# Weighted sums of a windowed attention: from pairs of units by parity to single units with up to four query blocks per matmul

## The chip, the cores and the metric

The kernel runs on one core of a Trainium2 chip. The metric is the time of one execution in device microseconds (us). The kernel before took 880.48 us in the median of three runs (876.16, 880.61 and 880.48).

## The reference

An attention with a window of 128 keys and a linear bias for each head, over 8 batches of 8 heads, 576 positions and 64 features, is followed by a two-layer network with an exact GELU. Cut to what matters:

```python
scores = (q @ k.T) / sqrt(64)                    # per batch and head, 576 x 576
scores = where(0 <= i - j < 128, scores - slope[h] * (i - j), -1e9)
attn   = softmax(scores)                         # in float32
x      = (attn @ v).transpose(0, 2, 1, 3).reshape(4608, 512)
out    = gelu(x @ w_in) @ w_out                  # w_in 512 x 2048, w_out 2048 x 512
```

## The kernel before, in words

**Units.** One unit is one batch `b` and one pair of heads `hp`, so a batch has four units. The 576 queries are cut into nine blocks of 64, and so are the keys. A query block `j` sees the key blocks `j-2`, `j-1` and `j` alone. `scores` (line 617 is its matmul) writes the products of one unit into PSUM, `biased` (line 643, VectorE) scales them and adds the bias, `softmax` takes maxima (VectorE), exponentials (line 730, ScalarE), sums, the division by them (line 740, GpSimd) and a float16 copy (line 742, ScalarE); `low_weights` (line 749, VectorE) makes the float16 remainder, and a transposing DMA from SyncE's queue puts both into the tile `et` of the unit, keys on the partitions. Every number is a sum of a high and a low float16 part, so each product takes three terms.

**Weighted sums.** `weigh` multiplies `et` with the values `vbuf` of one unit: key pair `kb` (two key blocks, 128 partitions) serves the query blocks `2kb` to `2kb+3`. One head is 64 columns of weights, so the two heads of a unit go to two halves of the PE array and run side by side. It takes up to two query blocks in a matmul (64 or 128 columns) and is used for batches 0 to 2. `weigh_two` (line 849) serves batches 3 to 7: it takes two units at once, one query block in each matmul, sorted by the parity of the block. Where half of the 128 keys of a key pair are outside the window it uses 64 partitions alone, so four such matmuls run side by side. It needs four PSUM banks at a time (three in batch 7) and the `et` of both units, and it has 192 matmuls with 192 loads of weights, for each of ten pairs of units.

**What leaves.** `leave` and `leave_two` bring the sums to the network's input `x`: a scaled float16 copy on ScalarE (lines 890 and 874) and the remainder on VectorE (`low_part`, line 302). Nine blocks of 64 do not fit a token tile of 512, so the sums of a batch go to two tiles, `t = b` and `t = b + 1`, which are called parts 0 and 1.

**The network.** Tile `t` of 512 tokens has sixteen feature blocks `h` (line 917; for tiles 4, 5, 6 and 8 seven products on sums of halves instead, `u` and `v`, line 1288 and others), GELU, and then four output blocks `o` (line 964).

**What sets the order.** Every instruction of every engine stands in an order written out by hand. `ORDER` holds the steps of tiles 0 and 1, `LATER` those of tiles 2 to 6 (with batches 3 to 7): a token such as `5Y0` runs the task `Y0` of tile `t = 5` (batch 6) to its next `yield`. `LATER_BANKS` gives each PSUM tile its bank, `LATER_ROOMS` each output room. Engines take their instructions in that order, and so does SyncE's DMA queue. The tasks of the weighted sums are `Y` and `X` in `later_tasks`:

```python
        for n in range(2):
            two = unit(b, 2 * n), unit(b, 2 * n + 1)
            made.update({f"Y{n}": weigh_two(*two), f"X{n}": leave_two(*two)})
```

Of the kernel before, what the change touches and what calls it, by code (L numbers as in the profile page):

```python
# [18 lines left out]
B, H, S, D = 8, 8, 576, 64  # L19
# [81 lines left out]
2gs K 2V 2S0 2gs 2V 2V 2gs K 2H0 3gs 2V 2H0 2B0 K 2H0 3gs 3gs 2B0 2B0 2H0 K 2H1 2B0 2B0 2g0 K 2B0 2H1 2M00 K 2H1 2B0  # L101
2H1 K K 2H2 2g1 2H2 2M00 2H2 2B0 2H2 2v 2H3 2B0 2g2 2g0 2H3 2g1 2H3 K 2H3 2M00 2M01 2H4 2g2 2H4 2g0 K 2H4 2g1 2g3 2H4
K 2g2 2H5 K 2H5 2g4 2v 2v 2v 2v 2v 2v 2S1 2g3 2M00 2v 2v 2v 2v 2g4 2g3 2H5 K 2H5 2M00 2B1 2M00 2g4 2H6 2B1 2g5 2B1 2H6
2M00 2v 2H6 2B1 2B1 2B1 2H6 2M00 2M01 2M10 2B1 2M00 2H7 2M00 2H7 2M00 2B1 2M00 2H7 2v 2M01 2v 2M00 2v 2v 2M01 2v 2g5
2H7 2v 2v 2M01 2v 2B1 2H8 2g5 2M00 2H8 2M01 2M11 2g6 2H8 2M01 2N00 2M01 2H8 2H9 2g7 2N00 2M01 2H9 2g8 2M01 2H9 2M01 K
2g6 2H9 2M01 2H10 2H10 2M10 2N01 2S2 2g7 2g6 2M10 2N01 2H10 2M10 2g8 2H10 2B2 2g9 2H11 2g7 K 2H11 2g8 2H11 2g10 2B2
2H11 2g9 2M10 2B2 2H12 2g10 2g9 2H12 2B2 K 2H12 2B2 2g11 2B2 2H12 2g10 2B2 K 2H13 2B2 2H13 2g12 2M20 2g11 2H13 2M10
2g12 2g11 2H13 K 2H14 2g12 2g13 2H14 K 2M10 2H14 2M10 K 2H14 2M11 2M10 2H15 2g13 2H15 2M10 2g13 2H15 2M10 2g14 2H15
2M10 2M10 2o0 2B2 2M21 2g15 2g14 2M10 4gs 2g15 2g14 2M11 2o0 2g15 2N10 2M11 2M11 4gs 2N10 K K 2o0 2M20 2M20 2M20 2M11
2M20 2o0 2M20 2M21 2M11 K 2M20 2M21 2M21 2M20 2M11 2M21 2M11 2M21 2M11 2M21 2o1 2k0 2M11 K 2M11 K 2N11 2M20 2S3 2N11  # L110
2M20 2M20 2o1 2B3 2M20 2M20 2B3 2B3 2Q 2M20 K 2k0 2B3 2B3 2M21 2N20 2M21 2o1 2B3 2M21 2M30 2M21 K 2M21 2B3 2B3 2o1 K
2B3 2M30 2M30 2M30 2N21 2M30 2Y0 2k1 2M31 2M30 2q 2M30 2M30 2M30 2M30 2o2 2M30 2N20 2M30 2M31 2M30 2M31 2M31 2M31 2o2
2X0 2N21 2M31 2M31 2M31 2X0 2M31 2X0 2X0 2M31 2X0 2X0 2X0 2M31 2Q 2M30 2X0 2o2 2X0 2X0 2N30 2M31 2X0 2N30 2X0 2N31 2o2
2o3 2q 2k2 2N31 2k1 2q 2q 2o3 2k2 2q 2q 2q 2q 2q 2q 2q 2q 2q 2q 2q 2q 2q 2q 2q 2o3 2q 2q 2Y1 2q K 2o3 2X1 3U 2X1 2X1
3H0 K 2X1 3H0 2k3 2X1 2X1 3H0 2X1 K 2k3 2X1 3H0 K 2X1 2X1 3H1 2X1 3g0 K 2X1 3U 3H1 K 3H1 3H1 3S0 3g1 4gs 3V 3H2 3B0
3g0 3V K 3H2 3B0 3g1 3H2 3H2 3B0 3H3 3g2 3V 3g0 3B0 3H3 K 3V 3B0 3H3 3B0 3H3 3M00 3B0 3g2 3S1 3g3 K 3B0 3M00 3g1 3H4
3B0 3g3 3H4 3B1 3M00 3H4 3M01 K 3M00 3H4 3B1 3M00 3B1 K 3H5 3M00 3g2 3B1 3g4 K 3H5 3B1 3B1 3H5 K 3M00 3H5 3g3 3B1 3M01
3g4 3H6 3B1 3M00 3H6 3M10 3B1 3M00 3H6 3M00 3g5 3M00 3g4 3H6 3M00 3M11 3H7 3M00 3H7 3v 3g6 3g5 3H7 3M00 3g6 3H7 3M01
3H8 3H8 3N00 3H8 3M01 3H8 3M01 3g5 3N00 3g7 3H9 3M01 3g6 3H9 3M01 3v 3v 3v 3M01 3v 3H9 3v 3v 3M01 3v 3g8 3v 3H9 3M01
3v 3v 3M10 3v 3M01 3v 3H10 3v 3g7 3v 3v 3v 3H10 3v 3v 3g8 3v 3H10 3g7 3M01 3H10 3g8 3M10 3H11 3M10 3N01 3M10 3H11 3M10  # L120
3N01 3H11 3M11 3M10 3M10 3H11 3M11 3M10 3M11 3M10 3H12 3M11 3M10 3H12 3M10 3g9 3M11 3M11 3M10 3H12 3M11 3M11 3H12 3M11
3H13 3g10 3M11 3g9 3g11 3H13 3g10 3M10 3g9 3H13 3g11 3H13 3M11 3g10 3H14 3g12 3H14 3g11 3g13 3g12 3H14 3N10 K 3g13
3H14 3H15 3g14 3H15 3N11 3S2 3N10 3g14 3g12 3H15 K 3H15 3g13 3o0 3g15 3N11 K 3g14 3g15 3o0 3B2 5gs K 3g15 3B2 K 3B2
5gs K 3o0 3B2 3B2 K 3B2 3M20 K K 3o0 3M20 3M20 3B2 3B2 3M20 K 3S3 3M20 3k0 3M20 3B2 3k0 K 3B3 3Q 3M21 3Y0 3B3 K 3B3
3M21 K 3M20 3M21 3M20 3B3 3B3 3M21 3M20 3B3 3M21 3M20 3o1 3M30 3M20 3X0 3M20 3M20 3M21 3X0 3M30 K 3M21 3X0 3M20 3M21
# [44 lines left out]
"""  # L170
LATER_BANKS = (
    "0124356701245673014567231047562314076523047651320475631204756230147563201475623014765231047625130745"
    "2136074523167043516270315640723150467320541673205146371423605712436750124736501437620143765210463527"
    "10635420763541"
)
LATER_ROOMS = (
# [1481 lines left out]
```

## Time and profile before

| what | value |
|---|---|
| three runs, median | 880.48 us (876.16 to 880.61) |
| the profiled execution's own time | 883.64 us |
| its span in the trace | 881.8 us |
| PE busy | 853.3 us (97%), 8580 matmuls and as many loads of weights |
| DVE, ACT, POOL busy | 699.9, 626.0, 285.8 us |
| matmuls of `weigh_two` | 1920, of two forms |
| matmuls of `weigh` | 480 in float16 (batches 1 and 2), 144 in float32 (batch 0) |

PE is TensorE's matmuls, PEld its loads of weights, DVE is VectorE, ACT ScalarE, POOL GpSimd and SP SyncE. A matmul's time in the trace is that from its start to its modelled end, so matmuls overlap in it. What one costs in a stream is the distance from start to start. "Issue" as the cause of an idle time means that the engine waited for nothing that the profile shows. The row "q8 instruction" of the DMA queues is the traffic that brings PE its instructions.

### The profile page before, as it was taken

The page shows a single profiled execution, that of the slowest core. Times are in us where ns is not written, and L with a number is a line of the kernel's source. Part 1 is how long each engine was busy: PE and PEld are TensorE (multiplying, and loading weights), DVE is VectorE, ACT ScalarE, POOL GpSimd, SP SyncE. Part 2 cuts the span into 40 slices and gives each one's busy share as a digit, 9 for nine tenths or more (in the row PEclk, how much of TensorE's full clock was granted, in tenths as well). Part 3 has the DMA queues.
Part 4 walks back from the last instruction along what each step waited for, and adds up shares of the span by engine and source line. Part 5 has one row for each costly group of instructions (what it writes and reads, how often), then busy time and mean ns, then how long its engine had stood idle before and what let it go on. Part 6 is the DMA issues. An engine that isn't in the chain of part 4 may idle for free.

```text
span 881.8 us, 21037 instructions
## 1 busy us (share of the span) xinstructions
PE 853.3 (97%) x8580; PEld 520.5 (59%) x8580; DVE 699.9 (79%) x1294; ACT 626.0 (71%) x1234; POOL 285.8 (32%) x481
## 2 busy tenths in 40 slices
PE   6999999999999999998999998999899999999998
PEld 4654445544554455444468545875487554588887
DVE  6999899999887765879687976889868999932871
ACT  7999779897677975794769683878486647722850
POOL 1010000122055861868515362556344610000000
PEclk9999999999999999999999999999999999999999
DMA  9765744544541388326743665465532440021201
GB/s 311 266 204 183 275 117 109 156 138 79 121 128 49 76 174 181 96 55 168 198 161 87 206 132 161 126 193 121 174 109 55 88 112 13 29 79 38 96 1 48
DMA packets 178064, 112.76 MB, mean 128 GB/s; under 512 B 134064, under 2 KB 156720, under 8 KB 175792
## 3 DMA queue, kind: packets, MB, share of 16 engines
q1 hardware_dynamic: 177968, 111.43, 45.2%
q8 instruction: 67, 1.10, 0.5%
q14 instruction: 29, 0.24, 0.1%
HBM read 63.31 MB, written 13.63 MB: 87 GB/s over the span
## 4 chain that ended last, share of the span: by engine, by line
PE 51%; DVE 23%; ACT 12%; DMA 7%; issue 4%; POOL 4%; SPq 0%; ACTq 0%; DVEq 0%; POOLq 0%
PE o L964 14%; PE u L1288 7%; PE h L917 6%; PE v L1288 5%; PE u_out L1390 4%; DVE g L302 3%; ACT s L730 3%; DVE s L643 3%; PE u L1186 2%; PE av L849 2%; PE sc L617 2%; DVE nmax L726 2%; DMA raw<-w_out 2%; PE v L1186 2%; DVE e_main L302 2%
## 5 line engine op out<-in xcount | busy, mean ns | idle before, releaser
L917 PE MATMUL h<-x,wi 128*128 128x512 f16 x960 | 213.4, 382 | 3.7 <-ACT g L938 2.1
L964 PE MATMUL o<-wo,g 128*128 128x512 f16 x864 | 193.3, 381 | 0.5 <-issue 0.5
L964 PEld LDWEIGHTS <-g 128*128 128x128 f16 x1152 | 111.1, 98 | 135.1 <-issue 3.7
L917 PEld LDWEIGHTS <-wi 128*128 128x128 f16 x960 | 93.1, 98 | 119.1 <-issue 9.7
L730 ACT ACTIVATE s<-s,nmax 128x192 f32<-128x192 f32 x252 | 111.4, 443 | 16.6 <-DVE nmax L726 16.3
L740 POOL TENSOR_SCALAR s<-s,z 128x192 f32<-128x192 f32 x180 | 89.5, 514 | 53.1 <-DVE z L734 40.5
L643 DVE SCALAR_TENSOR_TENSOR s<-sc,cs,bias_h 128x384 f32<-128x384 f32 x112 | 67.1, 607 | 4.2 <-PE sc L617 3.7
L964 PE MATMUL o<-wo_first,g 128*128 128x512 f16 x288 | 66.2, 380 | 0.5 <-issue 0.5
L649 POOL MEMSET s<- 64x128 f32 (+1 forms) x112 | 19.2, 172 | 146.3 <-DVE s L643 123.9
L1288 PEld LDWEIGHTS <-t 128*128 128x128 f16 x576 | 56.1, 98 | 6.8
L726 DVE TENSOR_REDUCE nmax<-s 128x5 f32<-128x960 f32 (+1 forms) x56 | 58.2, 1042 | 2.3 <-POOL s L649 2.0
L617 PE MATMUL sc<-kbuf,qbuf 64*64 64x192 f16 (+3 forms) x1656 | 49.9, 252 | 8.8 <-ACT qbuf L518 4.4
L961 PE MATMUL o<-zo,g 128*128 128x512 f32 x128 | 58.4, 609 | 0.0
L942 POOL TENSOR_SCALAR g<-g,sg 128x512 f16<-128x512 f32 x48 | 41.4, 869 | 52.2 <-DMA q<-qp 26.7
L742 ACT CAST e_main<-s 128x960 f16<-128x960 f32 (+1 forms) x40 | 36.3, 909 | 29.0 <-POOL s L740 22.5
L749 DVE TENSOR_TENSOR e_main<-s,e_main 128x960 f16<-128x960 f32 (+1 forms) x40 | 44.8, 1119 | 11.6 <-ACT e_main L742 11.4
L302 DVE SCALAR_TENSOR_TENSOR g<-g,sg,g 128x512 f16<-128x512 f32 x48 | 43.1, 919 | 7.5 <-POOL g L942 7.2
L730 ACT ACTIVATION_READ_ACCUMULATOR s<-s,nmax 128x1 f32 x252 | 47.2, 187 | 0.0
L1288 PEld LDWEIGHTS <-wi 128*128 128x128 f16 x432 | 41.9, 98 | 5.6
L938 ACT ACTIVATE g<-h,gs 128x512 f32<-128x512 f32 x48 | 31.5, 685 | 14.4 <-DVE g L302 10.8
L961 PEld LDWEIGHTS o<-zo,g 128*128 128x128 f32 x128 | 24.4, 194 | 28.2 <-issue 25.9
L617 PEld LDWEIGHTS <-qbuf 64*64 64x64 f16 x1512 | 30.4, 107 | 16.9 <-issue 15.9
(277 smaller groups left out, 1658.9 us busy)
## 6 DMA issues: line engine op xcount, KB each, us to landing
t<-stored SPq DMA_DIRECT2D x12, 1024.0 KB, 5.1
v<-vp SPq DMA_DIRECT2D x32, 320.0 KB, 5.5
out<-ob SPq DMA_DIRECT2D x34, 256.0 KB, 2.4
raw<-w_in SPq DMA_DIRECT2D x8, 1024.0 KB, 10.6
raw<-w_out SPq DMA_DIRECT2D x8, 1024.0 KB, 8.2
q<-qp SPq DMA_DIRECT2D x7, 1152.0 KB, 5.9
k<-kp SPq DMA_DIRECT2D x7, 1152.0 KB, 8.5
stored<-sums SPq DMA_DIRECT2D x8, 512.0 KB, 3.1
```

The lines of the kernel that those rows point to most:

```text
L302: return nc.vector.scalar_tensor_tensor(out=dst, in0=src, scalar=scale, in1=high, op0=ALU.mult, op1=ALU.subtract)
L617: done = nc.tensor.matmul(ps[bank][o, n, gap:W], a, m[:, gap:W], start=(i == 0 and (n == 0 or b > 0)), stop=(i == len(terms) - 1 and b > 0 ...
L643: yield nc.vector.scalar_tensor_tensor(out=s[:, bank[0] : bank[0] + k, :], in0=ps[bank][:, 0:k, 0:W], scalar=cs, in1=bias.broadcast_to([P, ...
L726: yield nc.vector.tensor_reduce(out=nmax[:, r], in_=s[:, r], axis=AX.X, op=ALU.max, negate=True)
L730: yield nc.scalar.activation(s[:, i, :], s[:, i, :], AF.Exp, bias=nmax[:, i : i + 1], accum_out=z[:, i : i + 1])
L740: yield nc.gpsimd.tensor_scalar(to, s[:, i], z[:, i : i + 1], 1.0, op0=ALU.mult, op1=ALU.mult)
L749: yield nc.vector.tensor_tensor(out=e[:, r, 1, c], in0=st.s[:, r], in1=e[:, r, 0, c], op=ALU.subtract)
L917: done = nc.tensor.matmul(ph, wi[n][:, a, cc, k * P : (k + 1) * P], x[:, cc, b, :], start=(i == 0), stop=(i == 3 * NCC - 1),)
L942: yield nc.gpsimd.tensor_scalar(g[:, r, 0], g32, gsg[t, n], 1.0, op0=ALU.mult, op1=ALU.mult)
L961: done = nc.tensor.matmul(o, g[:, r, c], zo[n][:, n % 2, k * DM : (k + 1) * DM], start=(fc == first), stop=(fc == last))
L964: done = nc.tensor.matmul(o, g[:, r, a, c], wo[n][:, b, k, :], start=(fc == first and i == 0), stop=(fc == last and i == 2),)
L1288: done = nc.tensor.matmul(ps[:, k * HT : (k + 1) * HT], w(a, i)[:, k * P : (k + 1) * P], m(b, i), start=first and n == 0, stop=True, skip_ ...
```

## The change

`weigh_two`, `leave_two` and `parity_blocks` are gone, and `weigh` and `leave` serve all batches, one unit at a time. From batch 1 on `weigh` takes four query blocks in one matmul of 256 columns where all four of a key pair belong to the same part and block 8 is not among them. Elsewhere it takes one or two, as before. The tasks `Y0` to `Y3` and `X0` to `X3` are now single units, and `LATER`, `LATER_BANKS` and `LATER_ROOMS` are new. `ORDER` and `PSUM_BANKS` are as they were.

```diff
@@ LATER, LATER_BANKS, LATER_ROOMS (new throughout; the first line of each table)
-2gs K 2V 2S0 2gs 2V 2V 2gs K 2H0 3gs 2V 2H0 2B0 K 2H0 3gs 3gs 2B0 2B0 2H0 K 2H1 2B0 2B0 2g0 K 2B0 2H1 2M00 K 2H1 2B0
+2gs K 2V 2S0 2gs 2V 2V 2gs K 2H0 3gs 2V 2H0 2B0 K 2H0 3gs 3gs 2B0 2B0 2H0 K 2H1 2g0 2B0 2B0 K 2B0 2H1 2M00 K 2H1 2B0
...
@@ weigh
+        k = 1 if b < EXACT else 2
+
+        def at(ei, slot, h, j):
+            g = 4 if j == 8 else (NEVEN if j % 2 else 0) + 2 * h + j // 4
+            half = h if j == 8 else half_of(b, h, j)
+            return et[:, (g * k + ei) * 2 + slot, half * QB : half * QB + QB]
+
         for part in parts:
...
             for kb in range(NKB):
-                for slot, j0 in ((1, 2 * kb), (0, 2 * kb + 2)):
-                    js = [j for j in (j0, j0 + 1) if j in blocks]
-                    if js:
-                        jobs.append((kb, slot, js))
+                js = [j for j in range(2 * kb, 2 * kb + 4) if j in blocks]
+                if b < EXACT or len(js) < 4 or 8 in js:
+                    cuts = [[j for j in js if j // 2 == kb + n] for n in range(2)]
+                    jobs.extend((kb, cut) for cut in cuts if cut)
+                else:
+                    jobs.append((kb, js))
             terms = ((None, 0),) if b < EXACT else ((0, 0), (0, 1), (1, 0))
...
                 for h in range(2):
                     r = slice(h * D, h * D + D)
...
+                    places = [at(ei, int(j // 2 == kb), h, j) for j in js]
+                    steps = [[places[m].offset - places[0].offset, 2] for m in (2, 1) if m < len(js)]
                     done = nc.tensor.matmul(
-                        av[r, (j - blocks[0]) * QB : (j - blocks[0] + len(js)) * QB],
+                        av[r, (js[0] - blocks[0]) * QB : (js[-1] + 1 - blocks[0]) * QB],
                         v32s[b][:, hp, kb, r] if b < EXACT else vbuf[:, vi, hp, kb, r],
...
             yield done
-
-    def weigh_two(one, two):
...
@@ later_tasks
-        for n in range(2):
-            two = unit(b, 2 * n), unit(b, 2 * n + 1)
-            made.update({f"Y{n}": weigh_two(*two), f"X{n}": leave_two(*two)})
+            made.update({f"Y{k}": weigh(st), f"X{k}": leave(st)})
```

How instructions move is shown at three places. Names such as `av5_2` are batch 5, unit 2.

The first is PE in batch 5, at the first weighted sums of unit 2, in the kernel before; the two numbers behind `av5_2` are the part's tile and the parity.

```order
L964 LDWEIGHTS g4_1_6252
L964 MATMUL o4_3_7365<-wo2_1886,g4_1_6252 128x512
L849 LDWEIGHTS vbuf_94
L849 MATMUL av5_2_5_0_7400<-et5_2_7282,vbuf_94 64x64
L849 LDWEIGHTS vbuf_94
L849 MATMUL av5_2_5_0_7400<-et5_2_7282,vbuf_94 64x64
L849 LDWEIGHTS vbuf_94
L849 MATMUL av5_2_6_1_7403<-et5_2_7282,vbuf_94 64x64
```

In the changed kernel the same unit has rows like these in its second part:

```order
L798 LDWEIGHTS vbuf_94
L798 MATMUL av5_2_6_6863<-et5_2_6719,vbuf_94 64x128
L798 LDWEIGHTS vbuf_94
L798 MATMUL av5_2_6_6863<-et5_2_6719,vbuf_94 64x256
L798 LDWEIGHTS vbuf_94
L798 MATMUL av5_2_6_6863<-et5_2_6719,vbuf_94 64x256
```

All 192 matmuls of a pair had 64 columns; now one unit has 60 (batches 3 and 5), 42 (batches 4 and 6) or 48 (batch 7) of 64, 128 and 256 columns. The ten bursts of 192 become fifteen: each unit by itself in batches 3 and 4 and for the first two of batch 5, and two units back to back for the other five. Output matmuls `o` stand between the bursts.

The second place is ACT at the start of tile 3, whose input `x3` takes the last sums from `av3_2` (before) and `av3_3` (now). The rows before:

```order
L545 ACTIVATE qbuf_91<-q32_4_3992,scq4_4356 128x2304
L545 ACTIVATE kbuf_92<-k32_4_4300,scq4_4356 128x2304
L874 ACTIVATE x3_2962<-av3_2_3_0_4407,cx3_3_3180 128x2x3x64
L505 ACTIVATE vbuf_94<-v32_4_3199,scv4_3394 128x2560
L874 ACTIVATE x3_2962<-av3_2_3_1_4408,cx3_3_3180 128x2x2x64
```

And now:

```order
L545 ACTIVATE qbuf_91<-q32_4_4037,scq4_4246 128x2304
L545 ACTIVATE kbuf_92<-k32_4_4053,scq4_4246 128x2304
L818 ACTIVATE x3_2890<-av3_3_3_4301,cx3_3_3084 128x320
L505 ACTIVATE vbuf_94<-v32_4_3103,scv4_3297 128x2560
```

One copy of five blocks stands ahead of the split of the values `vbuf`, where before the copy of the odd blocks stood behind it.

The third is SyncE's queue in tile 2, with the loads of batch 4's queries and keys, before:

```order
L524 DMA q32_4_3992<-qp 128x4x576
L978 DMA out_0<-ob2_0_3904 128x512
L1072 DMA stored1_104<-sums1_1_3845 128x2048
L753 DMA_TRANSPOSE et3_2_4265<-e_main_95 128x20x128
L753 DMA_TRANSPOSE et3_2_4265<-e_main_95 128x16x128
L524 DMA k32_4_4300<-kp 128x4x576
L753 DMA_TRANSPOSE et3_3_4321<-e_main_95 128x20x128
```

And now:

```order
L906 DMA out_0<-ob2_0_3881 128x512
L753 DMA_TRANSPOSE et3_2_3985<-e_main_95 128x20x128
L753 DMA_TRANSPOSE et3_2_3985<-e_main_95 128x16x128
L524 DMA q32_4_4037<-qp 128x4x576
L524 DMA k32_4_4053<-kp 128x4x576
L906 DMA out_0<-ob2_1_4030 128x512
L753 DMA_TRANSPOSE et3_3_4147<-e_main_95 128x20x128
```

The load of the queries has moved behind both transposes of unit 2, right ahead of that of the keys.

## Rows read from the trace of the kernel before

**Rows 1.** The page, part 1: busy time, share of span, instructions.
```profile
PE 853.3 (97%) x8580; PEld 520.5 (59%) x8580; DVE 699.9 (79%) x1294; ACT 626.0 (71%) x1234; POOL 285.8 (32%) x481
```

**Rows 2.** Windows of line 849, bursts: start:end, length, PE busy, PEld busy, clock, DMA, GB/s.
```profile
325.38:328.09 2.71, 2.71 (x192) 2.62 (x192) 1.00 0.97 383
410.44:415.86 5.42, 3.36 (x192) 2.89 (x192) 1.00 0.48 155
439.92:443.69 3.77, 2.89 (x192) 2.71 (x192) 1.00 0.21 74
514.23:518.49 4.26, 2.90 (x192) 2.72 (x192) 1.00 0.02 4
534.13:539.64 5.51, 3.27 (x192) 3.07 (x192) 0.89 0.71 236
624.72:629.38 4.66, 2.90 (x192) 2.69 (x192) 1.00 0.59 155
```

**Rows 3.** Timeline of PE behind bursts: start, length, form, count, idle time before and cause.
```profile
416.94 0.39 PE L964 MATMUL o<-wo_first,g 128*128 128x512 f16 x1 [0.48 <-issue]
538.64 1.06 PE L849 MATMUL av<-et,vbuf 128*64 128x64 f16 x32 [2.24 <-issue]
630.73 1.47 PE L964 MATMUL o<-wo,g 128*128 128x512 f16 x6 [0.54 <-issue]
```

**Rows 4.** Windows from the start into three of the stalls, PE alone: matmuls so far.
```profile
0.00:442.50 442.50, 423.70 (x3917) 0.99 0.56 154
0.00:517.50 517.50, 497.42 (x4812) 0.99 0.55 153
0.00:537.50 537.50, 515.84 (x5068) 0.99 0.56 153
```

**Rows 5.** DMA queues: packets, MB, share; the whole span, then 440 to 442.9 us.
```profile
q8 instruction: 67, 1.10, 0.5%
...
q8 instruction: 1, 0.02, 2.2%
```

**Rows 6.** Windows, all engines, behind the longest stall: clock is third from the end.
```profile
539.30:541.90 2.60, 2.60 (x21) 1.15 (x17) 0.61 (x2) 2.48 (x2) 0.00 (x0) 0.50 0.57 143
```

**Rows 7.** Timeline of PE: weighted sums of batches 1 and 2 and what follows each.
```profile
145.29 3.00 PE L795 MATMUL av<-et,vbuf 128*64 128x128 f16 x132
148.22 1.13 PE L961 MATMUL o<-zo,g 128*128 128x512 f32 x2
156.58 1.60 PE L795 MATMUL av<-et,vbuf 128*64 128x64 f16 x66
158.11 1.25 PE L917 MATMUL h<-x,wi 128*128 128x512 f16 x5
229.18 2.91 PE L795 MATMUL av<-et,vbuf 128*64 128x128 f16 x108
232.02 1.25 PE L964 MATMUL o<-wo,g 128*128 128x512 f16 x5
```

**Rows 8.** Timeline of PE in tile 4: full-array matmuls of 256 columns.
```profile
452.78 1.49 PE L1288 MATMUL u<-x,wi 128*128 128x256 f16 x12
454.10 1.47 PE L1288 MATMUL v<-x,wi 128*128 128x256 f16 x12
```

**Rows 9.** Timeline of PE: output matmuls ahead of the burst at 325.38.
```profile
319.67 5.78 PE L964 MATMUL o<-wo,g 128*128 128x512 f16 x26
```

**Rows 10.** Timeline of PE: the waits for data in tiles 3 to 6.
```profile
353.93 0.59 PE L917 MATMUL h<-x,wi 128*128 128x512 f16 x2 [0.84 <-ACT x L874]
412.03 0.22 PE L849 MATMUL av<-et,vbuf 64*64 64x64 f16 x4 [1.31 <-DVE s L643]
626.98 2.46 PE L849 MATMUL av<-et,vbuf 64*64 64x64 f16 x154 [1.76 <-DMA et<-e_main]
```

**Rows 11.** DMA issues, 320 to 342 us: KB, us to landing.
```profile
k<-kp SPq DMA_DIRECT2D x1, 1152.0 KB, 7.9
```

**Rows 12.** DMA issues, 485 to 502 us, with queries and keys issued together.
```profile
k<-kp SPq DMA_DIRECT2D x1, 1152.0 KB, 9.8
```

More of the change, by code (lines that the diff above doesn't have):

```diff
@@ L106 @@
[L106 to L125, printed above, removed]
@@ new lines @@
+3g9 3H13 3M10 3g11 3H13 3g10 K 3H14 3M11 3H14 3g12 3H14 3g13 3H14 3g11 3M11 3H15 3N10 3g14 3M11 3H15 3H15 3N10 3M11
+3H15 3g12 3M11 3S2 3g13 3g12 3g14 3o0 3g15 3B2 3N11 3B2 3g15 3B2 3N11 3g13 3B2 K 3o0 3B2 3B2 3g14 3B2 K 3B2 3g15 3S3 K
+3M20 3o0 K 3B3 3M20 K 5gs 5gs 3B3 3B3 K 3M20 3B3 3B3 3B2 3Y0 3M21 K K 3Y0 3M20 3o0 3M20 3M20 3B3 3M21 3M20 3M21 3M30
+3M21 K 3M21 3Y1 3X0 3k0 3Y1 K 3M30 3M20 3M30 3M21 3k0 3X0 K 3o1 3M30 3Q 3M21 3M30 K 3M30 K 3X0 3M30 3X1 3X0 3M20 K
+3M20 3o1 3M30 3X1 3X1 3M20 3X1 3o1 3M20 3M20 3M21 3M20 3M21 3M21 3q 3N20 3M21 3o1 3N20 3B3 3B3 3M30 3M30 3M21 3B3 3M30
@@ new lines @@
+3M30 3N21 3o2 3M30 3M31 3N21 3Z0 3M31 3M31 3o2 3M31 3M31 3Z0 3M30 3M31 3Q 3M31 3M31 3M31 3N30 3M31 3o2 3N30 3M31 3Z0
+3M31 3Z0 3N31 3o2 3Z0 3q 3N31 3Y2 3k2 3Y2 3o3 3X2 3q 3q 3q 3q 3k1 3q 3q 3q 3q 3q 3q 3q 3q 3q 3k2 3q 3q 3q 3k1 3q 3X2
+3Y3 3Y3 3o3 4T1 3X2 3q 3q 3o3 3X3 3q 3Z0 4U 3Z0 3o3 3X2 4T0 3X3 3Z1 3X3 4S0 3k3 3k3 3X3 410 3Z1 4B0 3Z1 420 4B0 4a0
+4B0 3Z1 4B0 3Z1 411 4a0 3Z1 421 4a1 3Z1 4a0 4U 460 4a0 461 4c0 450 4a1 4c1 4T2 4B0 4a1 4B0 470 4M00 4a1 4B0 451 4B0
+4d0 4M00 4B0 4d0 471 4M01 4a0 4M00 440 4d1 4a1 4M00 4d1 4M00 430 4T3 4e0 5gs 441 4c0 4c0 4e0 431 4e1 4c0 4e0 4M00 412
@@ L174 @@
-    "10635420763541"
+    "0124356701245673014562731045267341502647130264753016472530165473201654732016574321056742105374216507"
+    "3241650734215604721356475123047651230452173645217036542013675403167254031756204715632047156203457621"
+    "0345672134560721"
 )
 LATER_ROOMS = (
-    "0120120120120120120120120120120120120120120120120120121021021021"
+    "0120120120120120120120120120120120120120120102012012012012012012"
 )
@@ L777, in weigh @@
             for kb in range(NKB):
-                for slot, j0 in ((1, 2 * kb), (0, 2 * kb + 2)):
-                    js = [j for j in (j0, j0 + 1) if j in blocks]
-                    if js:
-                        jobs.append((kb, slot, js))
+                js = [j for j in range(2 * kb, 2 * kb + 4) if j in blocks]
[4 more added lines that the diff above has]
+                    jobs.append((kb, js))
             terms = ((None, 0),) if b < EXACT else ((0, 0), (0, 1), (1, 0))
-            k = 1 if b < EXACT else 2
             todo = [(vi, ei, job) for vi, ei in terms for job in jobs]
-            for n, (vi, ei, (kb, slot, js)) in enumerate(todo):
+            for n, (vi, ei, (kb, js)) in enumerate(todo):
                 for h in range(2):
                     r = slice(h * D, h * D + D)
-                    j = js[0]
-                    half = half_of(b, h, j)
-                    g = 4 if j == 8 else (NEVEN if j % 2 else 0) + 2 * h + j // 4
-                    if j == 8:
-                        half = h
-                    base = et[:, (g * k + ei) * 2 + slot, half * QB : half * QB + QB]
-                    steps = [[NEVEN * 2 * k * P, 2]] if len(js) == 2 else []
+                    places = [at(ei, int(j // 2 == kb), h, j) for j in js]
+                    steps = [[places[m].offset - places[0].offset, 2] for m in (2, 1) if m < len(js)]
                     done = nc.tensor.matmul(
-                        av[r, (j - blocks[0]) * QB : (j - blocks[0] + len(js)) * QB],
+                        av[r, (js[0] - blocks[0]) * QB : (js[-1] + 1 - blocks[0]) * QB],
                         v32s[b][:, hp, kb, r] if b < EXACT else vbuf[:, vi, hp, kb, r],
-                        bass.AP(tensor=base.tensor, offset=base.offset, ap=[list(base.ap[0])] + steps + [[1, QB]]),
+                        bass.AP(tensor=places[0].tensor, offset=places[0].offset, ap=[list(places[0].ap[0])] + steps + [[1, QB]]),
                         start=(n == 0), stop=(n == len(todo) - 1), skip_group_check=True,
@@ L801, in weigh @@
             yield done
-    def parity_blocks(b, part, odd):
-        return [j for j in blocks_of(b, part) if j % 2 == odd]
-    def weigh_two(one, two):
-        b, pair = one.b, (one, two)
-        k = 1 if b < EXACT else 2
-        banks = [(part, odd) for part in range(2) for odd in range(2) if parity_blocks(b, part, odd)]
-        for part, odd in banks:
-            one.av[part, odd] = bank_of([P, TT], "att" if b else "mm", f"av{one.u}_{b + part}_{odd}")
-        where = {j: (part, odd, n) for part, odd in banks for n, j in enumerate(parity_blocks(b, part, odd))}
-        left = dict.fromkeys(((part, odd, h) for part, odd in banks for h in range(2)), 0)
-        todo = []
-        def job(rows, st, u, h, vi, ei, kb, slot, j):
-            part, odd, n = where[j]
-            g = 4 if j == 8 else (NEVEN if odd else 0) + 2 * h + j // 4
-            half = h if j == 8 else half_of(b, h, j)
-            c = slice(h * D, h * D + D)
-            at = (u * len(parity_blocks(b, part, odd)) + n) * QB
-            left[part, odd, h] += 1
-            todo.append((
-                (part, odd, h), one.av[part, odd][c, at : at + QB],
-                v32s[b][rows, st.hp, kb, c] if b < EXACT else vbuf[rows, vi, st.hp, kb, c],
-                st.et[rows, (g * k + ei) * 2 + slot, half * QB : half * QB + QB],
-            ))
-        terms = ((None, 0),) if b < EXACT else ((0, 0), (0, 1), (1, 0))
-        each = [(st, u, t) for u, st in enumerate(pair) for t in terms]
-        low = [(st, u, t, j // 2, 1, j) for st, u, t in each for j in range(0, NB, 2)]
-        high = [(st, u, t, (j - 3) // 2, 0, j) for st, u, t in each for j in range(3, NB, 2)]
-        for n, (st, u, t, *at) in enumerate(low):
-            for h in range(2):
-                job(slice(0, D), st, u, h, *t, *at)
-            if n < len(high):
-                st, u, t, *at = high[n]
-                for h in range(2):
-                    job(slice(D, P), st, u, h, *t, *at)
-        for st, u, t in each:
-            for j in range(1, NB):
-                for h in range(2):
-                    job(slice(0, P), st, u, h, *t, (j - 1) // 2, j % 2, j)
-        started = set()
-        for key, o, a, m in todo:
-            left[key] -= 1
-            done = nc.tensor.matmul(o, a, m, start=key not in started, stop=left[key] == 0, skip_group_check=True)
-            started.add(key)
-        yield done
@@ L853, in leave_two @@
-    def leave_two(one, two):
-        b, hp = one.b, one.hp
-        for part in range(2):
-            t = b + part
-            for odd in range(2):
-                js = parity_blocks(b, part, odd)
-                if not js:
-                    continue
-                at, n = b * S + js[0] * QB - t * TT, len(js)
-                av = one.av[part, odd][:, 0 : 2 * n * QB].rearrange("p (u n k) -> p u n k", u=2, n=n)
-                c = cx[b, t]
-                def dst(a, us):
-                    base = x_tile(t)[:, hp + us[0], a, at : at + QB]
-                    units_ = [[2 * TT, 2]] if len(us) == 2 else []
-                    return bass.AP(
-                        tensor=base.tensor, offset=base.offset,
-                        ap=[list(base.ap[0])] + units_ + [[2 * QB, n], [1, QB]],
-                    )
-                yield nc.scalar.activation(dst(0, (0, 1)), av, AF.Copy, scale=c)
-                for u in range(2):
-                    yield low_part(dst(1, (u,)), av[:, u], c, dst(0, (u,)))
```

108 lines of the change are left out of this document (58 added, 50 removed).

## Prediction

> **What bounds the kernel now.** I read the page's busy times first: PE is at work in 97% of the span [rows 1], so the time is PE's stream plus the moments in which it stands still. Next come the windows of the weighted sums, which are what the change rewrites. Each of the ten bursts of `weigh_two` has the same 192 matmuls. Five take 2.71 us, as the first row of [rows 2]; the other five, all shown there, take 3.77 to 5.51. So 2.71 is the price and the rest is standing still. The timeline then names what ended each standstill. In three of the bursts (439.92, 514.23 and 534.13; the last is shown) and twice shortly behind one it is "issue" [rows 3], otherwise it is data [rows 10].
>
> What is behind "issue"? The windows from the start of the program into three such stalls count the matmuls so far: 3917, 4812 and 5068 [rows 4]. The steps between them are 895 and 256, that is 7 x 128 less one and 2 x 128. A matmul and its load of weights are two instructions, so these stalls lie whole multiples of 256 instructions apart. The queue that brings instructions moved 67 packets in all, one of them at the stall of 442 us [rows 5], and PE's 2 x 8580 instructions [rows 1] divided by 67 are 256. I read the stalls as PE reaching the end of what it has been sent. In a burst 256 instructions last 128 x 2.71 / 192 = 1.8 us; in a stream of full matmuls they last much longer, and there the same borders cost nothing.
>
> The Trainium skill speaks against this reading ("Runtime: NRT & Kernel Launch", section "Instruction fetch mechanics"): it says that instructions arrive in blocks of 256 while the current block executes, and that crossing a block's border is mostly hidden because instructions are issued more slowly than blocks are filled. The trace agrees on the block and not on the hiding; by the rule the stalls would have another cause and the term for them below would be nought, which is rival C.
>
> **The change, part by part.**
>
> *Weighted sums on PE.* Before, 10 x 2.71 = 27.1 us. For the new form the float16 sums of batches 1 and 2 are the model, since they already run unit by unit with both heads side by side [rows 7]. A burst of 132 matmuls takes 148.22 - 145.29 = 2.93, one of half as many 158.11 - 156.58 = 1.53, so a burst costs 2 x 1.53 - 2.93 = 0.13 beside its matmuls. By the code, the 66 are 15 pairs of 128 columns and 18 of 64, and the 108 that take 2.84 are 42 and 12. Two equations (15a + 18b = 1.40, 42a + 12b = 2.71) give 0.0555 us for a pair of 128 columns and 0.0315 for one of 64. Pairs of 256 columns are not in the trace. A full-array matmul of 256 columns takes (454.10 - 452.78) / 12 = 0.110 [rows 8], just under two pairs of 128, so the lower end is 0.109 for a pair; the upper end is twice that, if its heads did not run side by side. I take 0.109, as the pairs of 128 do run so. A unit of batch 3 or 5 (18 pairs of 64 columns, 9 of 128, 3 of 256) then costs 1.39, one of batch 4 or 6 (6, 9, 6) 1.34, one of batch 7 (12, 6, 6) 1.37. Four of each: 27.3. Fifteen bursts at 0.13 add 2.0. Entering a burst costs too: the 26 output matmuls ahead of one took 325.38 - 319.67 = 5.71 up to its start [rows 9], about 0.1 more than 26 x 0.216. Five more bursts make 0.5. Together 29.8 against 27.1: **+2.7 us**. Batches 1 and 2 go from 480 to 384 matmuls over the same columns; 48 pairs of 256 at 0.109 for 96 of 128 at 0.0555 give **-0.1**.
>
> *Instruction stalls.* The bursts that stood still on "issue" exceed 2.71 by 1.06, 1.55 and 2.80 [rows 2]; behind two others PE idled 0.48 and 0.54 [rows 3]. After the longest, an idle time of 2.24, the granted clock is 0.50 until 541.9 [rows 6], 1.2 instead of 2.4 GHz. The 2.26 us from the burst's end on hold half their work, another 1.13. Sum 7.6. Where does the new stream run out? At about 27.3 / 1008 = 0.027 us for a matmul, 256 instructions of weighted sums would last 3.5 us, and no burst has 128 matmuls: the longest has 120, and the other 8 are output matmuls of 0.216, so at least 4.8 us pass. The longest stall tells what is needed: 1.8 us of burst and 2.24 of idling, about 4.1. So I take all of it: **-7.6**. The ends are -7.6 and 0 (rival C).
>
> *Data waits.* The burst at 410.44 took 2.71 too long, as it needed four banks and waited for VectorE to empty scores [rows 10]. In the new order unit 0 of batch 4 needs two banks that older scores left, and unit 1 starts only 24 output matmuls (5.2 us) behind the last scores: **-2.7**, at worst 0. The copy for tile 3 that PE waited for (0.84) stood behind the values' split on ACT and now stands ahead of it. But SyncE's queue now sends batch 4's queries with its keys. Keys landed 7.9 us from issue alone [rows 11] and 9.8 beside queries [rows 12], and the keys' split stands ahead of that copy's remainder on VectorE. One gain, one loss of some 1 to 2 us: **0**. The last unit of batch 6 was 1.76 us late [rows 10]; from its scores to its sums it is 108 output matmuls and three units (28 us) instead of 132 and a pair (31), while VectorE has 40 remainders to make in batches 3 to 7 instead of 76: **0**, ends -1.8 and +3. Unit 0 of batches 3 and 5 moves some 14 and 19 us of PE's work forward, since it no longer waits for unit 1, and what then stands behind it on ScalarE and VectorE waits for its copy; on SyncE's queue stores and transposes change places by a row or two. For waits that the new order adds I take **+0.5**, ends 0 and +3. The network's matmuls and the end of the program are as they were.
>
> **Sum.** The profiled execution took 883.64 us (span 881.8): + 2.7 - 0.1 - 7.6 - 2.7 + 0.5 = 876.4. It stands 3.2 above the median of the runs shown, 880.48. About 2 of that I give to its longest stall, the only one that lowered the clock, which the sum already takes off; the other 1.2 I subtract. **875.2 us**, 0.6% under the median.
>
> **The rivals.** *B, the gain is given back.* PE arrives some 7 us earlier at the last units of batches 5 to 7, but their weights come from scores, exponentials, division, copy, remainder and a transpose, and one of these was late already [rows 10]. If that chain doesn't keep up, PE waits there for "DMA et" instead. For it: that very row. Against it: VectorE is busy 79%, ScalarE 71% [rows 1], and VectorE loses work. It gives back two thirds of 7.6, 5: 880.2.
>
> *C, the stalls are no instruction fetch*, or move to other borders: 875.2 + 7.6 = 882.8. Against it: the multiples of 256.
>
> *D, slower: the matmul of four blocks streams at half speed.* Its moving operand steps in two levels between runs of 64, and the trace shows one level only. 96 pairs in batches 3 to 7 and 48 in 1 and 2, each 0.109 more: + 15.7, 890.9. The balance tips against the change at (880.5 - 875.2) / 144 = 0.037 a pair. Against it: a pair of 128 in two runs costs half of a plain 256.
>
> **How the numbers follow.** Forecast 0.68, B 0.14, C 0.11, D 0.07. One half per cent of 880.48 is 4.4, about what a measurement of this kernel can tell from no change, so faster means under 876.1 and slower over 884.9. The forecast's own unknowns (up to 3 us late in batch 6, up to 3 of new waits, up to 3 less or more of stalls) put 0.46 of its 0.68 under 876.1 and the rest within; B and C lie within, D above: faster 0.46, same 0.47, slower 0.07. The likeliest case alone spans 868 to 881; taking in B and most of C, the range is 867.5 to 882.8.
>
> **What would show it.** Right: no burst of weighted sums with an "issue" idle time of over 0.3 us; bursts of 60 matmuls near 1.5 us, of 120 near 2.9; some 59 packets of instructions instead of 67; granted clock at full from 300 us on. Wrong: idle PE before a last unit by "DMA et" (B); "issue" still there (C); a burst of 60 matmuls over 1.8 us (D).

## The result and the profile after

The changed kernel takes **867.18 us** (median of 4 runs, 866.35 to 868.06), the kernel before 879.94 beside it (876.16 to 880.61). The ratio is 0.9864, with a 95% interval of 0.9832 to 0.9895. That is faster by 12.8 us where 5.3 were forecast, and 0.3 us below the low end of the range. The profiled execution took 866.36 us, with a span of 864.6.

The page of the changed kernel, the row that answers to [rows 1] and the row of the instruction queue, which answers to the first of [rows 5]:

```profile
PE 848.4 (98%) x7572; PEld 520.5 (60%) x7572; DVE 696.0 (81%) x1258; ACT 627.7 (73%) x1236; POOL 296.9 (34%) x481
q8 instruction: 59, 0.97, 0.5%
```

Windows of the weighted sums of the changed kernel (its line 798), one burst of each kind, with columns as in [rows 2]:

```profile
304.98:306.50 1.52, 1.52 (x60) 1.47 (x60) 1.00 0.00 0
400.92:402.39 1.47, 1.47 (x42) 1.42 (x42) 1.00 0.00 0
522.21:525.13 2.92, 2.92 (x120) 2.88 (x120) 1.00 0.18 62
608.94:612.04 3.10, 3.01 (x84) 2.88 (x84) 1.00 0.63 115
682.56:685.42 2.86, 2.86 (x96) 2.81 (x96) 1.00 0.24 92
```

PE is busy through every burst. Only the one at 608.94 is longer than its kind (the other of 84 matmuls takes 2.81): its transposed weights land a little late. From tile 2 on, the timeline of PE has one idle time of over 0.2 us left, shown here with the first matmuls of tile 3, which in [rows 10] waited for a copy and now run through:

```profile
269.90 11.81 PE L845 MATMUL h<-x,wi 128*128 128x512 f16 x54 [1.52 <-ACT g L866]
...
346.36 5.34 PE L845 MATMUL h<-x,wi 128*128 128x512 f16 x24
```

The two profiles differ by 17.3 us, more than the medians. Of this 3.9 lie ahead of tile 2, where the first layer's matmuls start at 255.20 and at 251.35 us, although nearly all of that part is the same program. A stage free of it is that from this start to PE's end: 623.3 us before, 609.4 after.

### The profile page after: what moved, and what is told of

The parts are those of the page before. It is cut to its first block, busy times and chain, and to the rows that moved or that the text cites. A ratio compares the mean times of both kernels' runs of the same rounds, so it can differ in the third digit from the quotient of the medians.

```text
span 864.6 us, 18999 instructions
## 1 busy us (share of the span) xinstructions
PE 848.4 (98%) x7572; PEld 520.5 (60%) x7572; DVE 696.0 (81%) x1258; ACT 627.7 (73%) x1236; POOL 296.9 (34%) x481
## 4 chain that ended last, share of the span: by engine, by line
PE 75%; DVE 13%; ACT 4%; DMA 4%; issue 3%; POOL 1%; SPq 0%; ACTq 0%; DVEq 0%; POOLq 0%
PE o L892 28%; PE h L845 13%; PE u L1216 7%; PE v L1216 5%; PE av L798 4%; PE u_out L1318 4%; PE sc L617 4%; PE u L1114 2%; PE v L1114 2%; PE z_out L1318 1%; PE x_out L1318 1%; PE y_out L1318 1%; PE v_out L1318 1%; DMA q<-qp 1%; DVE nmax L726 1%
## 5 line engine op out<-in xcount | busy, mean ns | idle before, releaser
L845 PE MATMUL h<-x,wi 128*128 128x512 f16 x960 | 211.2, 379 | 2.1 <-ACT g L866 1.5
L740 POOL TENSOR_SCALAR s<-s,z 128x192 f32<-128x192 f32 x180 | 96.0, 554 | 39.2 <-DVE z L734 23.7
L302 DVE SCALAR_TENSOR_TENSOR g<-g,sg,g 128x512 f16<-128x512 f32 x48 | 40.7, 864 | 9.8 <-POOL g L870 9.7
L798 PEld LDWEIGHTS <-vbuf 128*64 128x64 f16 x1392 | 40.1, 111 | 8.7 <-issue 7.7
L798 PE MATMUL av<-et,vbuf 128*64 128x128 f16 (+2 forms) x1392 | 42.4, 220 | 0.1
```

What stands on the lines that cost most here:

```text
L740: yield nc.gpsimd.tensor_scalar(to, s[:, i], z[:, i : i + 1], 1.0, op0=ALU.mult, op1=ALU.mult)
L798: done = nc.tensor.matmul(av[r, (js[0] - blocks[0]) * QB : (js[-1] + 1 - blocks[0]) * QB], v32s[b][:, hp, kb, r] if b < EXACT else vbuf[:, ...
L845: done = nc.tensor.matmul(ph, wi[n][:, a, cc, k * P : (k + 1) * P], x[:, cc, b, :], start=(i == 0), stop=(i == 3 * NCC - 1),)
```

## The experiments

**Do the idle times by "issue" hang on where an instruction stands in the program?** Run e1 puts 64 small matmuls ahead of the kernel before, and run e7 ahead of the changed one:

```diff
     with tc.manual_schedule(engines=None):
+        start_bank = psums[-1].tile([P, D], F32, tag="bank7", name="start", bufs=1)
+        for _ in range(64):
+            nc.tensor.matmul(start_bank, ident, ident[:, 0:D], start=True, stop=True)
         for step in ORDER.split():
```

> The kernel before with 64 small matmuls (128 instructions) put on PE ahead of the program's first score matmul, where PE waits for its first data anyway. Nothing else moves, so every border of 256 instructions falls 128 instructions earlier in the program. Theory A (PE runs out of instructions at borders of 256): the bursts that start near 440, 514 and 534 us, 3.77, 4.26 and 5.51 us long, fall to 2.71, and those near 325, 346, 606, 700 and 719 us, all 2.71, rise to 3.6 to 5.1 with an idle time by issue; the bursts near 410 and 625 gain one as well, beside or under their data wait. Seven stalls of about 1.6 for five: 882 to 889 us. Rival C (the stalls have another cause, tied to these bursts' data or place): the same three bursts stay long to 0.2 us, the five others stay at 2.71, and the time is 880 to 881.

Measured: 875.07 us (ratio to the kernel before 0.9963, 0.994 to 0.9985). The bursts of the padded kernel, line 849, without the one that first waits for banks at 408 us:

```profile
319.51:324.23 4.72, 2.90 (x192) 2.73 (x192) 1.00 0.75 263
344.15:348.56 4.41, 2.90 (x192) 2.73 (x192) 1.00 0.02 4
435.93:438.64 2.71, 2.71 (x192) 2.63 (x192) 1.00 0.26 97
509.82:512.53 2.71, 2.71 (x192) 2.62 (x192) 1.00 0.02 6
528.17:531.17 3.00, 2.89 (x192) 2.70 (x192) 1.00 0.17 31
596.81:599.52 2.71, 2.71 (x192) 2.62 (x192) 1.00 0.03 9
615.16:622.37 7.21, 4.42 (x192) 4.18 (x192) 0.69 0.66 156
694.02:697.40 3.38, 2.93 (x192) 2.73 (x192) 1.00 0.04 12
713.04:715.75 2.71, 2.71 (x192) 2.63 (x192) 1.00 0.03 6
```

The three long bursts of before (3.77, 4.26, 5.51) are at 2.71, 2.71 and 3.00, with no idle time by issue, and the first, second and eighth row, all 2.71 before, now have one. (The seventh waits 2.8 us for its weights and then runs at a lower clock.) Moving the program by 128 instructions moved the stalls, so rival C falls. Matmuls counted from the start into these stalls:

```profile
0.00:323.00 323.00, 311.61 (x2766) 0.99 0.55 162
0.00:347.50 347.50, 334.11 (x3022) 0.99 0.56 163
0.00:696.40 696.40, 677.86 (x7113) 0.99 0.53 148
```

Divided by 128 they leave 78, 78 and 73. The counts of [rows 4] leave 77, 76 and 76: the same border, though 64 of the matmuls are new. But I had expected seven stalls and a slower kernel, and the bursts at 596.81 and 713.04 stayed at 2.71. There the border lies in the burst too. What differs is when its packet came: in the trace of the DMA queues the packet that belongs to the border at 598.57 starts at 595.52, while PE is still on the output matmuls ahead of the burst, and that of the stall at 346.07 starts at 345.06, 0.91 us into its burst. Packets last 0.9 to 2.0 us, and at each of the eight stalls of the two profiles (five before, three here) PE resumes 1.2 to 1.6 us behind its packet's end. Matmuls counted along the trace say where the line runs. At the two borders without a stall the border ahead lies 13 and 17 matmuls into the burst, at the eight stalls 21 or more. So a border costs time when the request for its packet also goes out inside the burst, which happens some 20 matmuls ahead of the border before. My rule, the time of the last 256 instructions as they start, foresaw too many stalls, because it left this reading ahead out.

Run e3 asks for the reverse, stalls in the new order: one query block in each matmul.

```diff
-                if b < EXACT or len(js) < 4 or 8 in js:
+                if b > 2:
+                    cuts = [[j] for j in js]
+                    jobs.extend((kb, cut) for cut in cuts)
+                elif b < EXACT or len(js) < 4 or 8 in js:
```

> The changed kernel, with one query block in each matmul of the weighted sums of batches 3 to 7: the new order and the same columns, but 912 more matmuls. By the durations of 64 columns (15.9 ns) and merged blocks the sums take some 3 us more. Theory A: bursts of two units (some 200 matmuls in 3.2 us) run over the borders again; counting instructions from the program's start, five borders lie so that the 256 instructions ahead of them last only some 2 us, in batch 5's last burst, and both bursts of batches 6 and 7: 4.2 to 5.6 us each instead of about 3.2, and 875 to 879 us with the sums' own 3. Rival C (stalls belonged to the old form or the old order): no idle time by issue, bursts of two units near 3.2, 869 to 871.

Measured: 876.44 us (0.996, 0.9933 to 0.9988). Its five bursts of two units, line 801:

```profile
527.05:530.21 3.16, 3.16 (x192) 3.12 (x192) 1.00 0.11 40
595.56:600.03 4.47, 3.35 (x192) 3.19 (x192) 1.00 0.43 95
615.67:620.26 4.59, 3.35 (x192) 3.19 (x192) 1.00 0.73 228
690.78:695.24 4.46, 3.37 (x192) 3.22 (x192) 1.00 0.17 62
710.88:714.97 4.09, 3.37 (x192) 3.22 (x192) 1.00 0.01 4
```

The bursts that I named are long by 0.9 to 1.4 us, by issue; the one of batch 5 is not: there the border ahead lies only 1 matmul into the burst, as at the two of e1 it lay 13 and 17. The order is not what removed the stalls.

> The changed kernel with the same 64 small matmuls ahead of the program, so that its borders of 256 instructions fall 128 earlier. Theory A, as the padded kernel before refined it: PE's instructions come in time wherever a border falls in the new stream, since 256 instructions of it never last under 3.4 us. No idle time by issue over 0.3 us in or behind a burst, bursts of 60 matmuls at 1.52, of 84 at 2.82, of 120 at 2.92, and 867 within 2. Rival L (the changed kernel's borders only happen to lie well): one or more bursts 0.5 to 1.7 longer by issue, 868.5 to 872.

Measured: 866.13 us (0.9874, 0.9843 to 0.9905), no idle time by issue of over 0.2 us behind 300 us, bursts at 1.52, 2.82 and 2.92. So the new stream does not stall with its borders in either of two positions. Nor should it in a third: the least that 128 of its matmuls can take is 120 in 2.92 us and 8 output matmuls of 0.216, 4.65 us, while the longest block of 256 instructions that ended in a stall had lasted 2.6.

**Form or order?** Run e2 puts the new form into the old order: `Y0` and `Y1` weigh two units back to back, part by part, and `X0` and `X1` copy each of the four results in the places of the pair's copies.

```diff
     def weigh_two(one, two):
...
+        for part in range(2):
...
+            for u, st in enumerate((one, two)):
...
+                done = both(st, part, u, av)
         yield done
     def leave_two(one, two):
...
+            left = [leave(st, [part]) for st in (one, two)]
...
+            for task in left:
+                yield next(task)
+                yield next(task)
+                yield
```

> The new form of the weighted sums (up to four query blocks in one matmul, heads side by side) in the old order of tiles 2 to 6: where a pair of units stood, its two units stand back to back, their copies in the places of the pair's copies. If A holds, no burst idles by issue and 7.4 us go; the sums themselves cost 1 to 2 us more. Theory O (the rest of the change's gain is data waits that the new order removes): the waits near 271 (gelu), 352 (copy for tile 3), 365, 410 (banks) and 625 us (transposed weights) stay, 8 to 10 us in all, and the time is 873 to 877. Rival F (the form alone is the whole gain): 866 to 869, and these waits are gone or under 3 us in all. Rival C: still idle times by issue, 879 to 882.

Measured: 869.26 us (0.99, 0.9868 to 0.9933), 613.8 from tile 2 on. So by the medians the form alone brings 9.7 us and the order some 2 more. From tile 2 on, set against 619.0 us in a second profile of the kernel before (e8, below), it is 5.2 and 4.4. Neither O nor F is right as put. No burst idles by issue. The larger waits that are left, from the timeline of PE:

```profile
269.29 11.81 PE L910 MATMUL h<-x,wi 128*128 128x512 f16 x54 [2.02 <-ACT g L931]
287.49 10.52 PE L910 MATMUL h<-x,wi 128*128 128x512 f16 x48 [1.18 <-DVE s L643]
...
405.25 0.69 PE L833 MATMUL av<-et,vbuf 128*64 128x256 f16 x12 [0.71 <-DVE s L643]
406.43 1.89 PE L833 MATMUL av<-et,vbuf 128*64 128x128 f16 x60 [0.50 <-DVE s L643]
...
457.98 1.47 PE L1281 MATMUL u<-x,t 128*128 128x256 f16 x12 [0.78 <-ACT rooms L1323]
...
612.69 2.72 PE L833 MATMUL av<-et,vbuf 128*64 128x128 f16 x78 [0.45 <-DMA et<-e_main]
```

Set against [rows 10], the copy for tile 3 is no longer waited for, the late weights of batch 6 fell from 1.76 to 0.45, and of the wait for banks half is left. The new order takes all but the first of these away.

> The changed kernel with at most two query blocks in a matmul, in all batches: the new order, 288 more matmuls. Theory: columns, not matmuls, carry the time of the sums, and no border is reached in under 3.4 us; so the merging of four blocks is worth 0.3 to 1 us, 867.3 to 868.5, and no burst idles by issue for more than 0.4. Rival: merging four blocks is what makes the gain, 870 or more.

Run e4 (the test for `cuts` made `if True:`) gave 867.18 us (0.9882, 0.9848 to 0.9917), the changed kernel's own median, with bursts of 66 matmuls at 1.53 and of 132 at 2.94. The bursts of the changed kernel have 60 matmuls in 1.52 and 120 in 2.92, so four blocks in one matmul are worth 0.01 to 0.02 us a burst: the columns carry the time. Two had already made the stream sparse enough for the borders of this run, where the shortest block of 128 matmuls lasted 3.35 us. One that falls wholly into a burst of 132 would last 2.85, and no run tried that.

**Why did tile 3 stop waiting?** Run e6 puts the values' split ahead of the copy again.

```diff
-2X3 3U 2q K 3H0 ...
+3U 2X3 2q K 3H0 ...
```

> The changed kernel with one step moved back: ScalarE's high part of batch 4's values stands ahead of the copy of the last sums of batch 3 for tile 3, as in the kernel before. Theory: PE's first matmul of tile 3 (near 346 us) waits for that copy again, 0.8 to 1.6 us in all, 867.8 to 869. Rival: the wait before came from elsewhere (the pair's copies, four instead of two), and nothing changes: no idle time there, 867.2 within 0.6.

Measured: 866.76 us (0.9868, 0.9847 to 0.9888). ScalarE's rows and PE's start of tile 3 in e6:

```profile
345.31 2.41 ACT L505 ACTIVATE vbuf<-v,scv 128x2560 f16<-128x2560 f32 x1
347.63 0.51 ACT L818 ACTIVATE x<-av,cx 128x320 f16<-128x320 f32 x1
...
347.97 5.34 PE L845 MATMUL h<-x,wi 128*128 128x512 f16 x24
```

The split stands ahead, and PE does not wait: nothing changes, as the rival says, and ScalarE's order of split and copy is not the cause. The rival's reason, the form of the copies, is not shown by this. In the old form one copy holds every other query block of both units, so PE's matmuls on the third unit, from the seventh of tile 3 on, already need the second copy. Now the third unit has a copy of its own. But in e6 the late copy ends at 348.14, ahead even of the seventh matmul (347.97 + 6 x 0.216 = 349.27), and run e1, with the old copies in the old order, doesn't wait either. ScalarE and PE there, below ScalarE in the kernel before:

```profile
348.53 0.58 ACT L874 ACTIVATE x<-av,cx 128x384 f16<-128x384 f32 x1 [4.12 <-PE av L849]
...
351.15 5.34 PE L917 MATMUL h<-x,wi 128*128 128x512 f16 x24
```

```profile
346.42 2.21 ACT L545 ACTIVATE qbuf<-q,scq 128x2304 f16<-128x2304 f32 x1 [2.98 <-DVE scq L297]
348.54 2.20 ACT L545 ACTIVATE kbuf<-k,scq 128x2304 f16<-128x2304 f32 x1
350.64 0.56 ACT L874 ACTIVATE x<-av,cx 128x384 f16<-128x384 f32 x1
```

In e1 ScalarE stands ready when the burst ends at 348.56. In the kernel before it is still at the splits of batch 4's queries and keys, and its first copy starts 1.6 us behind the burst's end at 349.03. These splits start 5.2 us (before) and 5.4 us (e8) ahead of PE's first matmul of tile 3 where PE waits, and 6.8 to 6.9 (e2, e6, the changed kernel) and 11.1 (e1) where it does not. So the wait belongs to late splits. What makes them earlier in the new form, with the order old (e2) or new, stays open.

**What comes from one execution, not from the kernel?**

> The kernel before once more, for a second profile of the same program. Theory: the five idle times by issue stand at the same five places to 0.3 us each, since they hang on where instructions stand in the program; the waits for data at 98, 271, 352, 365, 410 and 625 us, which hang on when loads land, differ by 0.5 to 2 us each, and so does whether the granted clock falls behind the first two. From the start of tile 2's first layer to PE's end it is 618 to 624 us, 623.3 in the first profile. Rival: all waits are as before to 0.3 us.

Run e8 (the kernel before again, 877.00 us, 619.0 from tile 2 on), its idle times by issue in the timeline of PE:

```profile
412.86 2.33 PE L964 MATMUL o<-wo_first,g 128*128 128x512 f16 x10 [0.92 <-issue]
438.82 0.86 PE L849 MATMUL av<-et,vbuf 128*64 128x64 f16 x43 [0.88 <-issue]
513.68 0.57 PE L849 MATMUL av<-et,vbuf 128*64 128x64 f16 x24 [1.14 <-issue]
533.22 0.69 PE L849 MATMUL av<-et,vbuf 128*64 128x64 f16 x32 [1.12 <-issue]
624.03 7.30 PE L964 MATMUL o<-wo,g 128*128 128x512 f16 x33 [0.58 <-issue]
```

They are the five places of [rows 3] and [rows 2], but not the sizes: 2.24 became 1.12, without a fall of the clock, because the packet took 1.01 us instead of 1.92. The waits for data, which I had expected to vary, stayed nearly alike: 0.64 for the copy, 1.35 for banks, 1.90 for the weights, against 0.84, 1.31 and 1.76 in [rows 10]. Only the one for a gelu near 271 us fell from 2.13 to 1.56, and no half clock followed it.

> The changed kernel once more, for a second profile. From the start of tile 2's first layer to PE's end 609 to 612 us (609.4 in the first profile); the wait near 268 us is there again, 1.5 to 2.6 us, with or without a fall of the granted clock behind it, and no idle time by issue over 0.3 us in a burst.

Run e9: 866.42 us, 609.2 from tile 2 on, idle 1.37 at 270.03, and none by issue. As expected, but for the idle time, a little under the 1.5 that I had named.

**A version that beats both.** The wait near 268 us that all profiles of both orders show is VectorE's: its maximum over batch 4's values stands idle for their load, with the gelus' low parts behind it. Run e5 moves the step.

```diff
-... 2B0 2H2 2v 2H3 2B0 2g2 ...
+... 2B0 2H2 2H3 2B0 2g2 ...
...
-2H4 K 2H5 2g2 K 2H5 2v 2v 2g4 ...
+2H4 K 2H5 2g2 K 2H5 2v 2v 2v 2g4 ...
```

> The changed kernel with one step moved: the maximum over batch 4's values on VectorE, which waits for their load, stands some ten steps later, behind the low parts of tile 2's first three gelus instead of ahead of them. In the changed kernel's profile PE stands 1.52 us near 268 us for a gelu that waits for VectorE, and VectorE waits 3.8 us for that load. Theory: the wait goes (idle under 0.4 there), 865 to 866.5. Rival: the maximum takes 2.8 us of VectorE wherever it stands, and the next low parts or scores wait for it instead: 867 or more, with an idle time by DVE or ACT within 10 us of the old place.

Measured: 864.83 us (0.9848, 0.9825 to 0.987). Run beside the changed kernel:

> The changed kernel again, timed beside run e12 on the same chip. Theory: 866 to 868, and from the start of tile 2's first layer to PE's end 609 to 610 us.

> Run e5's kernel again beside the changed one: batch 4's maximum later. Theory: 1.5 us less than run e11, in the time (864.5 to 866.5) and from the start of tile 2's first layer to PE's end (607.5 to 608.2). Rival: what varies from run to run ahead of tile 2 is larger than this, and the two cannot be told apart in the time.

Measured: e11 866.50 (0.9869, 0.9845 to 0.9892), e12 864.72 (0.9846, 0.9821 to 0.9872); 609.0 and 607.7 from tile 2 on. The intervals against the kernel before overlap, but in the stage itself the wait is gone. VectorE in the changed kernel, then VectorE and PE in e12:

```profile
263.45 2.82 DVE L370 TENSOR_REDUCE stv<-v 128x1 f32<-128x2560 f32 x1 [3.77 <-DMA v<-vp]
```

```profile
261.18 2.65 DVE L302 SCALAR_TENSOR_TENSOR g<-g,sg,g 128x512 f16<-128x512 f32 x2
264.43 1.21 DVE L302 SCALAR_TENSOR_TENSOR g<-g,sg,g 128x512 f16<-128x512 f32 x1 [0.59 <-POOL g L870]
265.56 2.81 DVE L370 TENSOR_REDUCE stv<-v 128x1 f32<-128x2560 f32 x1
...
267.25 13.12 PE L845 MATMUL h<-x,wi 128*128 128x512 f16 x60
```

Three low parts go first, the load has landed by then, and PE does not stop.

> The kernel with batch 4's maximum later (run e5), and besides one output product of tile 0 moved ahead of batch 1's first scores, near 98 us, where the traces show PE waiting 0.6 to 1.2 us for a gelu that frees the scores' bank. Theory: that wait goes, and with it the chance that the granted clock falls behind it (1.6 us where it does): 862.5 to 864.5. Rival: the product waits for its own gelu there, and nothing is gained: 864.8 within 0.7.

Run e10 (e5 with an `O` of `ORDER` moved ahead of `S0`) gave 866.10 us (0.9869, 0.9845 to 0.9893). The product waited for its own gelu, and nothing was gained; the time is even above the rival's band of 864.1 to 865.5:

```profile
99.45 1.98 PE L889 MATMUL o<-zo,g 128*128 128x512 f32 x4 [1.02 <-ACT g L860]
```

## Why the prediction was right, and where it was off

- **The bound and the mechanism of the stalls: right.** They moved with the program (e1), came back with more instructions (e3), are gone with fewer (e2, e4) and stay gone with the borders in another position (e7). The Trainium skill's rule ("Runtime: NRT & Kernel Launch", "Instruction fetch mechanics") that crossing a border is mostly hidden agrees with the trace for streams of long matmuls, where no border shows an idle time by issue, and not inside the bursts and right behind them, where PE stood 0.5 to 2.2 us. The least time of 256 instructions in the new stream, put at 4.8 us, is 4.65, which changes nothing.
- **Weighted sums, +2.7: right.** The fifteen bursts of batches 3 to 7 take 4 x 1.52 + 4 x 1.47 + (2 x 1.52 + 2.92) + 2 x 2.81 + 2 x 2.86 = 29.3 us against 27.1, without the 0.29 of late weights; with 0.5 for entering five more bursts, 2.7. Rival D is out.
- **Instruction stalls, -7.6: the mechanism right, the size that of one execution.** In e8 the three bursts exceed 2.71 by 1.06, 1.33 and 1.31, and the idle times behind two others are 0.92 and 0.58, in all 5.2 by the prediction's way of counting, and the clock does not fall.
- **Data waits: the step that failed.** The banks' -2.7 came (with the order; e2 keeps half). The two zeros were wrong. The wait for the copy for tile 3 went, 0.9 to 1.1 us. The prediction weighed the copy's place against a later landing of the keys. The place does not matter (e6), and the keys did take longer, 9.0 us instead of 7.9, but were issued 22.4 us ahead of PE's first matmul of tile 3 instead of 18.3. Batch 6's late weights fell from 1.8 or 1.9 us of idling to 0.2 or less. Two smaller waits, 0.34 by "DVE s" near 365 us and 0.08 near 580, stood in no term. The +0.5 for new waits did not come. Why batch 6's weights are earlier is open: VectorE makes 36 remainders fewer, which I knew and gave no price, but no run changed that alone. Rival B, which would have lengthened this wait, has the wrong sign.
- **Sum.** An idle time costs PE 0.15 to 0.25 us more than the timeline shows, since it is counted from a modelled end that lies behind the next matmul's usual start (the burst that is 1.06 too long shows 0.88). Counted from start to start, PE loses in the second profile of before, from tile 2 on, 5.5 us by instructions, 2.7 by banks, 1.2 by the copy, 2.1 by late weights, 1.2 in three small waits near 289, 361 and 574 us and 1.7 by the gelu near 271: 14.4. The changed kernel loses 1.7 by that gelu and 0.3 by late weights. So 12.4 are gone and 2.7 come in for the sums, 9.7 in all, where 619.0 became 609.4, 9.6 less. The -0.1 lies ahead of tile 2. The first profile has 4.3 more: its longer stalls with their half clock, and a half clock behind the gelu near 271 us that is chance too (below).
- **The standing of the profiled run, -1.2**, was taken for luck of one place. The kernel before spreads from 875.4 to 885.9 in 23 runs, the changed one from 866.0 to 868.3 in its own, e9's and e11's: in the two profiles of before, 6.6 us apart, 4.3 lie from tile 2 on, in stalls that hang on a packet's time and in the clock.

## What to carry to other kernels

Count the instructions of a burst of short matmuls against the blocks in which they arrive: where two borders fall in one burst, the first of them some 20 matmuls or more behind its start, the engine stood still here, and fewer instructions over the same columns removed that, up to the point where the stream was sparse enough and not further. Before a wait for a copy is put down to its place or its form, look for a run in which the same copy is not waited for, and at all that stands ahead of it on its engine. Before pricing a wait from one profile, take a second one: the place of a stall can be fixed and its length be chance.

## What the runs showed of the hardware

An idle time of PE of 2 us near 268 us is followed by the half clock in one execution and not in another, and the longer one need not be the one that is: 1.98 us in e4 was, 2.02 in e1 and e2 was not. The windows of PE behind it in e2, whose idle time of 2.02 is shown above, and in e6, with e6's row of the timeline:

```profile
271.00:274.00 3.00, 3.00 (x15) 1.00 0.00 0
```

```profile
271.00:274.00 3.00, 3.00 (x9) 0.50 0.00 0
```

```profile
269.82 13.50 PE L845 MATMUL h<-x,wi 128*128 128x512 f16 x54 [2.04 <-ACT g L866]
```

The same 54 matmuls take 11.81 us in e2 and 13.50 here, so the clock at 1.2 instead of 2.4 GHz costs 1.7, nearly as much as the idle time itself. Also unexpected: a packet of instructions took 0.9 to 2.3 us over all traces, each the same 16 KB (0.97 MB in 59), and at every stall PE resumed no earlier than 1.2 us behind its end.
